# A redrawn order of 3657 operations and fewer early filler matmuls in clustered attention with a softplus feed-forward, on one core

## Chip, core and metric

The kernel runs on one core of one Trainium2 chip. The metric is the device time of one execution in microseconds, as the median of several runs. The core's engines take their instructions each from a queue of its own and wait for each other by semaphores: TensorE (PE, matmuls and transposes), VectorE (DVE), ScalarE (ACT), GpSimd (POOL), and SyncE (SP), which issues the DMAs.

## The reference

Four batches of eight heads, 768 rows of 64, attend within clusters: a row of q and a row of k see each other only if their nearest centroid out of 16 is the same. A feed-forward with softplus follows.

```python
q_assign = np.argmax(np.einsum('bhsd,hcd->bhsc', q_n, c_n), axis=-1)
k_assign = np.argmax(np.einsum('bhsd,hcd->bhsc', k_n, c_n), axis=-1)
mask = q_assign[:, :, :, None] == k_assign[:, :, None, :]
scores = np.where(mask, scale * np.matmul(q, k.transpose(0, 1, 3, 2)), -1000000000.0)
attn = np.exp(scores - np.max(scores, axis=-1, keepdims=True))
attn = attn / (np.sum(attn, axis=-1, keepdims=True) + 1e-09)
x = np.matmul(attn, v)                    # 3072 rows of 512 over all heads
h = x @ w_in                              # 512 -> 2048
g = np.maximum(h, 0.0) + np.log1p(np.exp(-np.abs(h)))
return g @ w_out                          # 2048 -> 512
```

## The kernel before

Numbers are split into a high and a low fp16 part, so that a product in fp32 quality is three fp16 matmuls (high by high, high by low, low by high). A split is two steps that occur all over the program: a cast (`cast`, recorded at L538) makes the high part, and a subtraction (`sub`, L528) makes the low one. `cast` can stand on ACT, DVE or POOL, `sub` on DVE or POOL. The weights arrive as 64-bit floats; `prep_weights` turns them into fp32 by integer steps on DVE and ACT (L662 to L683) and splits them (tiles wi and wo).

The work runs in 8 passes, a half of one batch's rows each (3 tiles of 128 rows for each of 8 heads). For each of 192 score tiles, `scores` does four matmuls (L1020), the negated row maximum on DVE (negm, L1036), the exponential on ACT (p, L1047) and then one of three ways of turning the weights: the first 24 tiles are transposed in fp32 on PE (pT, L1064, then ptf), 10 later ones on PE too (L1087 to L1095), and most of the others are split into phl (`cast`, `sub`) in pairs of tiles, which a transposing DMA on SP brings to pt. `attend` then multiplies with v (tile mbank; L1152 in fp32, L1156 to L1158 in fp16 parts); after the last tile of two heads DVE scales the result by the sums' reciprocals (rs, x, L1182 to L1191), and the result is split (xn) and turned into xT. `ffn1` (L1235 to L1237) makes h, `softplus` makes fg on ACT, DVE and POOL (L1262 to L1284) and splits it into gh, `ffn2` (L1318 to L1320) makes o, and `store` (L1334, L1338, then a DMA) writes it. The keys and queries of the first pass (kn, qn) are transposed on PE (kT, qT, L743) and copied from PSUM by ACT or DVE (`evict`, L519).

What sets the order is written out by hand. Each piece of work is a generator that yields its operations; `Order.run` takes the next code of the table SEQUENCE, its remainder modulo 1000 names the generator whose operation is recorded next, and its thousands name the engine where an operation offers a choice. So the table fixes both each engine's queue and who does each cast, subtraction and copy. The waits between engines follow from the tiles.

`Order` also keeps a clock of planned times. From it `warm` (L484 to L493) puts filler matmuls (128x120, into a bank that nobody reads) on PE where the plan has a gap: 0.9 of the gap in pieces of 52 ns before the plan's time 30000 ns, a share of WARM_SHARE later, where gaps over WARM_FROM alone count.

Of the kernel before, what the change touches and what calls it, by code (L numbers as in the profile page):

```python
# [35 lines left out]
WARM_SHARE = 0.65  # L36
# [368 lines left out]
def tile_cluster_attention__then__softplus_ffn(  # L405
# [80 lines left out]
    def warm(begin, end):  # L486

        ready, spot = min([(od.ev[b], b[1]) for b in od.idle] + [(od.mread, 9)])
        gap = end - max(begin, ready)
        if gap > (150 if begin < 30000 else WARM_FROM):  # L490
            out = idle if spot == 9 else ps_u.tile([P, 512], F32, tag=f"u{spot}", name="fill")[:, :WARM]
            for _ in range(int(gap * (0.9 if begin < 30000 else WARM_SHARE) / 52)):
                nc.tensor.matmul(out, eye, ones[:, :WARM], start=True, stop=True)  # L493
# [858 lines left out]
    first, begin = {}, []  # L1352
# [61 lines left out]
```

## Time and profile before

| what | us |
|---|---|
| median of 3 runs (838.05 to 838.40) | 838.29 |
| the profiled execution | 839.26 |
| its span, first to last instruction of the program | 837.5 |
| PE busy | 819.1 |
| DVE busy | 661.1 |
| ACT busy | 577.7 |
| POOL busy | 410.0 |

A busy time is the union of an engine's instructions; the matmuls' ends are modelled, so PE's is an upper one, and PE's fillers count as busy. The chain of work that ended last runs 74% of the span through PE, 8% through DVE, 7% through ACT and 5% through the transposing DMAs.

### The profile page before, as it was taken

How to read it: one execution, taken by the hardware profiler on the slowest of the kernel's cores; microseconds unless marked ns; L12 is line 12 of the kernel's file. 1: busy time of each engine (PE TensorE's matmuls, PEld its weight loads, DVE VectorE, ACT ScalarE, POOL GpSimd, SP SyncE). 2: the span in 40 equal slices, each digit the busy share in tenths (PEclk: the TensorE clock that was granted, in tenths of full speed). 3: DMA queues.
4: the chain of work that ended last, by engine and by line, in shares of the span. 5: the costliest groups of instructions: out<-in, count | busy, mean ns of one | idle time of the engine just before them, and what ended most of it. 6: DMA issues, size and time to landing. Idle time of an engine off the chain costs nothing.

```text
span 837.5 us, 19752 instructions
## 1 busy us (share of the span) xinstructions
PE 819.1 (98%) x8016; PEld 526.7 (63%) x8016; DVE 661.1 (79%) x1168; ACT 577.7 (69%) x977; POOL 410.0 (49%) x327
## 2 busy tenths in 40 slices
PE   9999989999999999999999999999999999999998
PEld 9788966655666666555565666656666666655553
DVE  7999999999898988889675788888777777534442
ACT  6999989987677758666676656667677587533230
POOL 3334445643554634563565455756566665421220
PEclk9999999999999999999999999999999999999999
DMA  9326887999989999999957999999999985500001
GB/s 328 117 95 141 232 168 190 197 216 191 191 173 181 180 192 190 190 204 174 192 105 108 174 189 201 189 203 207 185 182 181 163 161 113 98 23 13 26 1 38
DMA packets 377003, 131.93 MB, mean 158 GB/s; under 512 B 353360, under 2 KB 369744, under 8 KB 376912
## 3 DMA queue, kind: packets, MB, share of 16 engines
q1 hardware_dynamic: 376912, 130.67, 77.1%
q8 instruction: 62, 1.02, 0.5%
q14 instruction: 29, 0.24, 0.1%
HBM read 35.68 MB, written 6.29 MB: 50 GB/s over the span
## 4 chain that ended last, share of the span: by engine, by line
PE 74%; DVE 8%; ACT 7%; DMA 5%; issue 3%; POOL 2%; POOLq 0%; ACTq 0%; DVEq 0%
PE s L1020 11%; PE o L1318 8%; PE o L1319 8%; PE o L1320 8%; PE h L1235 8%; PE h L1236 8%; PE h L1237 8%; DMA pt<-phl 5%; PE mbank L1156 3%; PE mbank L1158 3%; PE mbank L1157 3%; PE mbank L1152 2%; DVE negm L1036 2%; ACT p L1047 2%; PE pT L1064 1%
## 5 line engine op out<-in xcount | busy, mean ns | idle before, releaser
L1047 ACT ACTIVATE p<-s,negm 128x768 f32<-128x768 f32 x188 | 168.7, 902 | 78.0 <-DVE negm L1036 70.3
L1036 DVE TENSOR_REDUCE negm<-s 128x1 f32<-128x768 f32 x192 | 181.1, 951 | 31.7 <-PE s L1020 28.2
L528 POOL TENSOR_TENSOR phl<-p,phl 128x768 f16<-128x768 f32 x81 | 138.2, 1711 | 79.4 <-ACT phl L538 37.5
L1235 PE MATMUL h<-xT,wi 128*128 128x384 f16 x512 | 166.7, 326 | 1.8 <-DVE fg L1273 1.2
L1237 PE MATMUL h<-xT,wi 128*128 128x384 f16 x512 | 166.8, 326 | 0.0
L1236 PE MATMUL h<-xT,wi 128*128 128x384 f16 x512 | 166.8, 326 | 0.0
L1020 PE MATMUL s<-kt,qt 128*128 128x384 f16 x768 | 156.0, 325 | 2.4 <-ACT p L1047 1.4
L1320 PE MATMUL o<-wo,gh 128*128 128x512 f16 x384 | 145.5, 379 | 0.0
L1319 PE MATMUL o<-wo,gh 128*128 128x512 f16 x384 | 145.5, 379 | 0.0
L1318 PE MATMUL o<-wo,gh 128*128 128x512 f16 x384 | 145.5, 379 | 0.0
L1284 POOL TENSOR_TENSOR fg<-fg,fa 128x384 f32<-128x384 f32 x68 | 74.3, 1094 | 109.8 <-ACT fa L1280 95.3
L1156 PE MATMUL mbank<-vb,pt 128*128 128x65 f16 x1008 | 108.9, 192 | 5.9 <-DMA pt<-phl 4.0
L1157 PE MATMUL mbank<-vb,pt 128*128 128x64 f16 x1008 | 108.9, 192 | 0.0
L1158 PE MATMUL mbank<-vb,pt 128*128 128x65 f16 x1008 | 108.6, 194 | 0.0
L1156 PEld LDWEIGHTS <-pt 128*128 128x128 f16 x1008 | 93.6, 98 | 18.7 <-DMA pt<-phl 7.1
L1157 PEld LDWEIGHTS <-pt 128*128 128x128 f16 x1008 | 93.0, 97 | 13.7 <-issue 2.4
L1020 PEld LDWEIGHTS <-qt 128*128 128x128 f16 x768 | 71.4, 98 | 47.9 <-issue 3.8
L1158 PEld LDWEIGHTS <-pt 128*128 128x128 f16 x1008 | 93.2, 97 | 0.0
L538 ACT CAST phl<-p 128x768 f16<-128x768 f32 x107 | 87.5, 832 | 7.9 <-DMA pt<-phl 6.6
L1266 ACT ACTIVATE fa<-h 128x384 f32<-128x384 f32 x79 | 38.7, 490 | 71.8 <-PE h L1237 65.3
L1279 ACT ACTIVATE fa<-fa 128x384 f32<-128x384 f32 x128 | 66.5, 524 | 27.0 <-DVE fa L1262 26.6
L528 DVE TENSOR_TENSOR phl<-p,phl 128x768 f16<-128x768 f32 x73 | 78.2, 1079 | 6.8 <-ACT phl L538 6.1
(174 smaller groups left out, 1466.2 us busy)
## 6 DMA issues: line engine op xcount, KB each, us to landing
wo<-in_moe_w_in_dram SPq DMA_DIRECT2D x16, 512.0 KB, 7.6
wo<-in_moe_w_out_dram SPq DMA_DIRECT2D x14, 512.0 KB, 4.1
rawk<-in_k_dram SPq DMA_DIRECT2D x16, 384.0 KB, 4.7
rawv<-in_v_dram SPq DMA_DIRECT2D x16, 384.0 KB, 4.2
rawq<-in_q_dram SPq DMA_DIRECT2D x16, 384.0 KB, 4.1
out_dram<-ot SPq DMA_DIRECT2D x24, 256.0 KB, 2.5
pt<-phl SPq DMA_TRANSPOSE x79, 6.0
wraw<-in_moe_w_out_dram SPq DMA_DIRECT2D x2, 512.0 KB, 4.6
```

The costliest lines, as they stand in the source:

```text
L528: [lambda e=e: e.tensor_tensor(dst, a, b, ALU.subtract) for e in (nc.gpsimd, nc.vector)],
L1020: nc.tensor.matmul(st[:, j, :SH], qt[:, s, i], kt[:, s, NT // 2 * j : NT // 2 * (j + 1)], start=(s == 0), stop=(s == 1),)
L1036: yield op("DVE", 950, lambda: nc.vector.tensor_reduce(negm, st[:, :, :SH], AX.XY, ALU.max, negate=True))
L1156: nc.tensor.matmul(av, pt[:, 0, c], vb[:, c, D : 2 * D + 1], start=(c == 0), stop=False)
L1157: nc.tensor.matmul(av[:, :D], pt[:, 0, c], vb[:, c, :D], start=False, stop=False)
L1158: nc.tensor.matmul(av, pt[:, 1, c], vb[:, c, D : 2 * D + 1], start=False, stop=(c == NT - 1))
L1235: nc.tensor.matmul(hp, w[0], x[0], start=(c == 0), stop=False)
L1236: nc.tensor.matmul(hp, w[0], x[1], start=False, stop=False)
L1237: nc.tensor.matmul(hp, w[1], x[0], start=False, stop=(c == NP - 1))
L1318: nc.tensor.matmul(po, g[0], wo[:, f, 0, 0], start=(f == f0), stop=False)
L1319: nc.tensor.matmul(po, g[0], wo[:, f, 0, 1], start=False, stop=False)
L1320: nc.tensor.matmul(po, g[1], wo[:, f, 0, 0], start=False, stop=(f == f0 + NF // 2 - 1))
```

## The change

SEQUENCE is another order of the same operations: 3657 codes in both, 3348 places of which differ. 445 codes choose the second engine of an operation where 459 did, 102 the third where 60 did. In `warm` the first gap (planned to begin before 2500 ns) is filled to 0.95 in pieces of 100 ns, and gaps up to 30000 ns to 0.75 instead of 0.9. The fillers go from 303 to 224, those ahead of PE's first transposes from 89 to 44. Everything else stays.

```diff
@@ -97,170 +97,170 @@
 SEQUENCE = [
-    0, 0, 0, 1, 0, 0, 0, 5, 0, 0, 0, 1, 2, 0, 3, 0, 4, 6, 5, 469, 0, 467, 0, 0, 468, 0, 433, 1001, 471, 8, 1, 0, 9,
+    1, 0, 0, 0, 0, 2001, 0, 0, 0, 5, 0, 0, 0, 0, 0, 2, 0, 3, 1001, 0, 5, 1, 1, 0, 468, 4, 1005, 0, 0, 469, 1, 0, 0,
...
@@ -489,7 +489,7 @@
         gap = end - max(begin, ready)
         if gap > (150 if begin < 30000 else WARM_FROM):
             out = idle if spot == 9 else ps_u.tile([P, 512], F32, tag=f"u{spot}", name="fill")[:, :WARM]
-            for _ in range(int(gap * (0.9 if begin < 30000 else WARM_SHARE) / 52)):
+            for _ in range(int(gap * (0.95 if begin < 2500 else 0.75 if begin < 30000 else WARM_SHARE) / (100 if begin < 2500 else 52))):
                 nc.tensor.matmul(out, eye, ones[:, :WARM], start=True, stop=True)
```

The first place is DVE's queue in the opening, from the last step of the centroids' norms to the first copies of transposed keys (cn and cb are the centroids' parts, kn the first two heads' keys, vb the values, kT the transposed keys in PSUM). Before:

```order
L591 TENSOR_SCALAR cn<-cf,crn 128x64
L594 MEMSET cb 128x192
L528 TENSOR_TENSOR kn_0_138<-rawk_124,kn_0_138 128x12x64
L596 CAST cb<-cn 128x64
L528 TENSOR_TENSOR vb_103<-rawv_128,vb_103 128x12x64
L596 CAST cb<-cn 128x64
L519 COPY kt_139<-kT_0_0_173 128x768
L597 TENSOR_TENSOR cb<-cn,cb 128x64
L921 SCALAR_TENSOR_TENSOR qn_2_0_151<-rawq_0_125,qn_2_0_151 128x6x64
L598 TENSOR_TENSOR cb<-cn,cb 128x64
L921 SCALAR_TENSOR_TENSOR qn_0_0_150<-rawq_0_125,qn_0_0_150 128x6x64
```

Now:

```order
L528 TENSOR_TENSOR kn_0_135<-rawk_124,kn_0_135 128x12x64
L591 TENSOR_SCALAR cn<-cf,crn 128x64
L594 MEMSET cb 128x192
L528 TENSOR_TENSOR vb_103<-rawv_128,vb_103 128x12x64
L596 CAST cb<-cn 128x64 x2
L597 TENSOR_TENSOR cb<-cn,cb 128x64
L598 TENSOR_TENSOR cb<-cn,cb 128x64
L519 COPY kt_136<-kT_0_6_215 128x768
L921 SCALAR_TENSOR_TENSOR qn_0_0_153<-rawq_0_125,qn_0_0_153 128x6x64
L921 SCALAR_TENSOR_TENSOR qn_2_0_154<-rawq_0_125,qn_2_0_154 128x6x64
```

The kn subtraction moves ahead of cn, the two cb subtractions ahead of the first copy out of PSUM, and that copy takes the second half of kT (kT_0_6), the first half being ACT's now.

The second place is DVE's queue at the 33rd to 35th row maximum (wo are weights in preparation, phl_3 a pair of tiles on its way to a transposing DMA). Before:

```order
L1036 TENSOR_REDUCE negm_4_2015<-s_4_2005 128x1
L519 COPY xT_1254<-xT_0_3_2102 128x384
L677 SCALAR_TENSOR_TENSOR wo<-wo 128x512
L683 SCALAR_TENSOR_TENSOR wo<-wo 128x512 x2
L528 TENSOR_TENSOR phl_3_2108<-p_2_3_2097,phl_3_2108 128x768
L528 TENSOR_TENSOR phl_3_2108<-p_2_4_2100,phl_3_2108 128x768
L1273 TENSOR_SCALAR fg_0_2146<-h_0_2110 128x384
L1036 TENSOR_REDUCE negm_5_2134<-s_5_2107 128x1
L1036 TENSOR_REDUCE negm_3_2154<-s_3_2136 128x1
```

Now:

```order
L519 COPY xT_1270<-xT_0_0_1975 128x384
L668 TENSOR_SCALAR wo<-wo 128x512
L519 COPY xT_1270<-xT_0_3_2013 128x384
L1036 TENSOR_REDUCE negm_4_1989<-s_4_1953 128x1
L677 SCALAR_TENSOR_TENSOR wo<-wo 128x512
L528 TENSOR_TENSOR kn_8_1982<-rawk_1897,kn_8_1982 128x12x64
L677 SCALAR_TENSOR_TENSOR wo<-wo 128x512
L1036 TENSOR_REDUCE negm_3_2074<-s_3_2066 128x1
L1036 TENSOR_REDUCE negm_5_2020<-s_5_1988 128x1
```

The two phl_3 subtractions left DVE, for POOL; a kn subtraction and a second copy to xT came to it.

The third place is POOL's queue in the third and fourth pass (phl a pair of tiles, gh and fg the feed-forward, xn attention's result). Before:

```order
L538 CAST gh_4_4488<-fg_4_4291 128x768
L528 TENSOR_TENSOR phl_1_4474<-p_15_1_4410,phl_1_4474 128x768
L528 TENSOR_TENSOR phl_3_4541<-p_8_3_4523,phl_3_4541 128x768
L1284 TENSOR_TENSOR fg_6_4625<-fg_6_4625,fa_12_4624 128x384
L1284 TENSOR_TENSOR fg_6_4625<-fg_6_4625,fa_13_4640 128x384
L528 TENSOR_TENSOR phl_5_4685<-p_9_3_4678,phl_5_4685 128x768
L528 TENSOR_TENSOR gh_6_4754<-fg_6_4625,gh_6_4754 128x768
L1284 TENSOR_TENSOR fg_7_4724<-fg_7_4724,fa_14_4723 128x384
L528 TENSOR_TENSOR phl_4_4793<-p_9_4_4787,phl_4_4793 128x768
```

Now:

```order
L1284 TENSOR_TENSOR fg_5_4413<-fg_5_4413,fa_11_4403 128x384
L538 CAST phl_5_4596<-p_9_3_4599 128x768
L528 TENSOR_TENSOR phl_5_4596<-p_9_3_4599,phl_5_4596 128x768
L538 CAST phl_5_4596<-p_8_5_4545 128x768
L528 TENSOR_TENSOR phl_5_4596<-p_8_5_4545,phl_5_4596 128x768
L528 TENSOR_TENSOR xn_2_4471<-x_13_2_4410,xn_2_4471 128x2x3x64
L1284 TENSOR_TENSOR fg_7_4651<-fg_7_4651,fa_14_4640 128x384
L528 TENSOR_TENSOR phl_4_4692<-p_9_4_4653,phl_4_4692 128x768
L538 CAST phl_4_4692<-p_9_5_4716 128x768
L528 TENSOR_TENSOR phl_4_4692<-p_9_5_4716,phl_4_4692 128x768
```

Where POOL did subtractions alone, it now often does a tile's cast and its subtraction one behind the other.

## Rows read from the trace of the kernel before

**Rows 1.** Busy us, share of the span and instructions of each engine.

```profile
PE 819.1 (98%) x8016; PEld 526.7 (63%) x8016; DVE 661.1 (79%) x1168; ACT 577.7 (69%) x977; POOL 410.0 (49%) x327
```

**Rows 2.** Stretches of the span; columns: us, busy (instructions) by engine, PE clock, DMA.

```profile
0.00:40.00 40.00, 36.50 (x594) 34.04 (x595) 34.20 (x120) 31.41 (x55) 14.35 (x22) 1.00 0.64 231
40.00:95.00 55.00, 54.19 (x502) 48.37 (x501) 54.38 (x102) 54.25 (x116) 22.29 (x22) 1.00 0.52 143
95.00:130.00 35.00, 32.09 (x385) 25.22 (x385) 34.14 (x59) 31.74 (x52) 15.81 (x14) 1.00 0.86 190
130.00:440.00 310.00, 303.70 (x3061) 187.83 (x3059) 275.12 (x458) 232.91 (x379) 164.87 (x125) 1.00 0.94 183
440.00:740.00 300.00, 298.96 (x2999) 184.07 (x2998) 227.16 (x378) 199.31 (x322) 176.18 (x133) 1.00 0.90 165
740.00:837.50 97.50, 93.64 (x485) 47.15 (x483) 36.09 (x54) 28.07 (x57) 16.46 (x14) 1.00 0.06 19
```

**Rows 3.** The same stretches for the fillers of L493 alone (PE, PEld).

```profile
0.00:40.00 40.00, 17.79 (x237) 15.96 (x237) 1.00 0.64 231
...
95.00:130.00 35.00, 4.12 (x66) 3.78 (x66) 1.00 0.86 190
```

**Rows 4.** What PE waited for: us in total, times, longest.

```profile
PE mbank L1156 <- DMA pt<-phl: 4.0, 7, 1.7
PE mbank L1156 <- DVE x L1191: 1.9, 2, 1.1
...
PE h L1235 <- DVE fg L1273: 1.2, 2, 0.9
```

**Rows 5.** Timeline of the opening: start us, length us, engine, line, operation [idle before].

```profile
1.84 7.58 PE L493 MATMUL fill<-ones,eye 128*128 128x120 f16 x89 [1.84 <-DVE ones L465]
...
5.87 0.89 DVE L528 TENSOR_TENSOR kn<-rawk,kn 128x768 f16<-128x768 f32 x1
...
8.12 0.94 ACT L917 ACTIVATE qn<-rawq 128x384 f16<-128x384 f32 x2 [1.58 <-DMA rawq<-in_q_dram]
...
9.26 0.50 PE L743 MATMUL kT<-eye,kn 128*128 128x128 f16 x6
...
9.59 1.79 PE L493 MATMUL mbank<-ones,eye 128*128 128x120 f16 x31
...
9.80 0.56 DVE L519 COPY kt<-kT 128x768 f16<-128x768 f16 x1 [1.97 <-PE kT L743]
```

**Rows 6.** Groups of instructions: count | busy us, mean ns | idle us before them.

```profile
L538 DVE CAST wi<-wo 128x512 f16<-128x512 f32 x7 | 3.6, 508 | 0.0
...
L528 DVE TENSOR_TENSOR phl<-p,phl 128x768 f16<-128x768 f32 x73 | 78.2, 1079 | 6.8 <-ACT phl L538 6.1 <-POOL phl L538 0.2
...
L683 DVE SCALAR_TENSOR_TENSOR wo<-wo 128x512 int32<-128x512 int32 x14 | 9.5, 688 | 0.1
...
L519 DVE COPY qt<-qT 128x384 f16<-128x384 f16 x4 | 1.4, 348 | 0.1
...
L538 DVE CAST phl<-p 128x768 f16<-128x768 f32 x26 | 17.1, 659 | 1.7 <-DMA pt<-phl 0.9 <-issue 0.8
...
L538 POOL CAST phl<-p 128x768 f16<-128x768 f32 x21 | 18.3, 874 | 20.6 <-ACT p L1047 11.0 <-DMA pt<-phl 7.3 <-issue 2.0
...
L1273 DVE TENSOR_SCALAR fg<-h 128x384 f32<-128x384 f32 x65 | 35.8, 550 | 27.9 <-ACT fa L1266 27.9
```

**Rows 7.** Timeline at 356 us on POOL and DVE, then PE's waits there.

```profile
355.95 1.64 POOL L528 TENSOR_TENSOR phl<-p,phl 128x768 f16<-128x768 f32 x1
...
356.02 2.39 DVE L528 TENSOR_TENSOR phl<-p,phl 128x768 f16<-128x768 f32 x1 [0.20 <-POOL phl L538]
...
358.74 0.56 DVE L1191 TENSOR_TENSOR x<-mbank,rs 128x384 f32<-128x384 f32 x1
...
PE mbank L1156 <- DVE x L1191: 1.1, 1, 1.1
```

**Rows 8.** Timeline of DVE's last instruction.

```profile
833.68 0.69 DVE L1338 SCALAR_TENSOR_TENSOR ot<-o,ot 128x512 f32<-128x512 f32 x1 [4.49 <-PE o L1320]
```

326 rows, old and new, of the table SEQUENCE are left out of this document.

## The prediction

> **What bounds the kernel now.** I read the busy times first, then the same busy times cut into stretches, then what TensorE (PE) waited for, then the timeline of the opening, and last single groups of instructions for durations. PE is busy 819.1 of 837.5 us [rows 1], so at most 18.4 us of idle time and whatever PE does that is not the program's own work can be won: 303 filler matmuls (L493), which are busy for 17.79 us in the first 40 us and 4.12 us between 95 and 130 us [rows 3]. The reader is to see in the stretches [rows 2] that the limit changes. In 0 to 40 us PE idles 3.5 us and fills 17.79. From 40 to 95 us PE (54.19 of 55), VectorE (DVE, 54.38) and ScalarE (ACT, 54.25) are all full. From 95 to 130 us DVE is full (34.14 of 35), ACT has 3.3 us free, and PE idles 2.9 and fills 4.12: DVE sets the pace. From 130 to 740 us PE is the limit, with 6.30 and 1.04 us idle; from 740 us on nothing stops it until the last matmul. GpSimd (POOL) is never the limit, 410.0 us busy in all. What PE waits for afterwards is spread over several names, none above 4.0 us in all [rows 4].
>
> The profiled execution took 839.26 us, 1.76 more than its span; the median of the runs is 838.29, 0.97 below it. I make the sum on the span and carry both differences along. A measurement of this kernel can tell about 0.2% from no change, 1.7 us.
>
> **The opening.** Before, PE runs 89 fillers from 1.84 to 9.2 us. The first kn subtraction on DVE starts at 5.87 and takes 0.89, so its transposes could start at about 6.9; they start at 9.26, when the fillers are through, and DVE idles 1.97 us before the copy of their result at 9.80 [rows 5]. The fillers were not covering a gap, they made one. The 89 took 7.58 us, 85 ns each; the next 31 took 1.79 us, 58 ns each: the first ones ran slower than the new count supposes now (100 ns each). The change puts 44 there: 44 x 0.085 to 0.100 = 3.7 to 4.4 us, ending near 6.2, ahead of the subtraction. The cast of kn moves from ACT to POOL (0.874 us for one of its size [rows 6]) with its load no earlier, so the subtraction still ends at about 6.9, and PE is free by then. DVE then has the two cb casts and subtractions done before the first kt copy. By the seventh row maximum (L1036) the order holds 126 DVE instructions in both kernels, worth the same, so nothing else moves here. Gain 9.26 - 6.9 = **2.4 us**. Bounds: 0, if the raw q load that ACT waits for until 8.12 [rows 5] paces everything behind it; 3.5, all of PE's idle time of this stretch.
>
> From 40 to 95 us I take nothing: PE is full there, and what it has lost by 40 us it carries on.
>
> **95 to 130 us.** Counted in the order up to its 34th row maximum, DVE goes from 264 to 257 instructions. Six wi casts leave it (6 x 0.508 = 3.0), two phl subtractions (2 x 1.079 = 2.2) and two weight steps of L683 (2 x 0.688 = 1.4); four copies to qt come (4 x 0.348 = 1.4) [rows 6]. That is 5.2 us off; the other kinds differ by one to three instructions each and I leave them at nothing. ACT does three more wi casts and three fewer wo casts, four fewer qt copies; it has 3.3 us free here. Most of what leaves goes to POOL, which idles more than half of this stretch (15.81 busy of 35) [rows 2]. DVE thus comes earlier by up to 5.2 us to the maxima on which the scores wait, and PE has 2.9 + 4.12 = 7.0 us to win. One of its waits, 1.7 us for a transposing DMA (part of the 4.0 us [rows 4]), starts from DVE's phl subtractions and shrinks only as far as those are earlier than PE. Bounds 0 (ACT takes over as the limit) and 5.2; I take the middle, **2.7 us**, for ACT's row of the stretch lies closest behind DVE's.
>
> **130 to 740 us.** Here 7.3 us of PE idle are left [rows 2]. Over the whole program DVE has 34 instructions fewer: 14 phl casts (14 x 0.659 = 9.2 us), 11 of L1273 (11 x 0.550 = 6.0) and the six wi casts (3.0) make 18.2, and the other kinds nearly cancel. POOL has 39 more, 26 of them phl casts (26 x 0.874 = 22.7 us) [rows 6], the rest at most as long each, so some 31 in all. POOL's idle half covers them. PE's waits that name a DVE instruction of this stretch, x L1191 1.9 and fg L1273 1.2 [rows 4], are 3.1 us; with DVE's load some 3% lower (18.2 of 661.1) I take off somewhat under half, **1.4 us**. Bounds: +5, most of the idle time gone, and -4, new waits of the same size in other places, since every engine's order was drawn anew. The order itself excludes neither.
>
> **The end** is the same on PE instruction for instruction from the last h groups on, and the last store still follows DVE's 0.69 us [rows 8]: nothing.
>
> Sum: 837.5 - 2.4 - 2.7 - 1.4 = 831.0 us of span, + 1.76 = 832.8 for such an execution, and 0.97 less for the median: **831.8 us**. With all bounds at once it would be 824.6 (3.5 + 5.2 + 5 off) to 842.3 (4 on); the forecast's own case, each term between half and one and a half of itself, is 828.5 to 835.
>
> **Rivals.**
> *Lock collisions on POOL's new pairs (slower).* Of 154 phl tiles POOL does cast and subtraction for 31 instead of 10. At 355.95 us POOL starts a 1.64 us subtraction and DVE, 0.07 us later, one that takes 2.39 instead of some 0.95; DVE's x (L1191) comes 1.44 us late and PE waits 1.1 [rows 7]. That is the price of one collision that reaches PE. The Trainium skill, SBUF — State Buffer, section "SBUF: two separate sides", describes the pair of ports that DVE and GpSimd share as an exclusive lock held for a whole instruction, so the loser stops altogether; the trace agrees, 2.39 against 1.64 + 0.95 less the head start of 0.07 = 2.52. By that rule alone, each of POOL's 39 more casts is one more chance to stop DVE. Against it: POOL holds both steps back to back, so fewer hand-offs between the two engines are needed (DVE cast then POOL subtraction falls from 17 tiles to 2), and in the profile most collisions end inside DVE's slack. Six more such waits (6 x 1.1 = 6.6) eat the forecast; ten more give 831.8 + 11 = 842.8, eight 840.6. Chance 0.10, at about 840.5.
> *The loads pace the opening and ACT the rest.* ACT's wait for raw q stays at 8.12 us and its rows of 40 to 95 us are as full as before; then neither term comes: 838. Chance 0.08.
> *The array's clock rises later.* With 45 fillers fewer in front, PE may stand still for half a microsecond before the first transposes; if the slow spacing of 85 to 100 ns lasts on into the transposes and the next 33 fillers, the opening's 2.4 us are given back: 834.2. The granted clock reads 1.00, the 2.4 GHz level, over the whole stretch [rows 2] and does not resolve this. The Trainium skill, TensorE: Matmul & The Clock Gate, section "Part 1: The HAM clock gate", speaks against the change here: activity releases the clock, an idle array gets the slow one. No row of this profile has PE standing idle between 1.84 and 9.26 us. Chance 0.08.
> *More of the waits go.* All of 95 to 130 us (5.2) and most of the later idle time (5) go with the opening's 2.4: 838.3 - 12.6 = 825.7. For it: DVE's load falls throughout. Against it: half of the waits are for DMAs. Chance 0.16.
>
> **How the numbers follow.** The forecast has 0.58. The range should leave out 2 in 10: from 825 to 838 it leaves out the slower rival (0.10), some 0.04 of the low one and the upper half of "nothing" with it, 0.04. Faster by over 0.2% (below 836.6): 0.58 + 0.16 + 0.08 = 0.82. Within 0.2%: the rival of the loads, 0.08. Slower: the collisions, 0.10.
>
> **What would show it.** Right: the first kT transposes at about 7 us instead of 9.26, DVE's 1.97 us wait gone, PE idle plus fillers between 95 and 130 us down from 7.0 to some 4, POOL near 440 us busy and DVE near 643. Wrong: DVE subtractions of 2 us and longer in greater number with PE's waits for DVE above 6 us in 130 to 740 (lock), the first transposes at 9 us (loads), or an even spacing of 100 ns among fillers after 8 us (clock).

## The result and the profile after

The changed kernel took **826.51 us** (median of 4 runs, 824.27 to 829.44) where the kernel before took 838.35 beside it: a ratio of 0.986, 95% interval 0.983 to 0.989. The prediction was 831.8 (825 to 838), faster by over 0.2%. The sign and the range hold, the range by 1.5 us; the gain is 11.8 us where 6.5 were forecast. Measured a second time (c1 below), the same kernel took 824.81 us beside 839.39, just outside the range.

The profiled execution is the fastest of the four, 824.27 us with a span of 822.2, so 15.3 us of span went. The page's busy line, and its chain of work that ended last, by engine:

```profile
PE 811.4 (99%) x7937; PEld 521.8 (63%) x7937; DVE 643.6 (78%) x1134; ACT 563.7 (69%) x972; POOL 445.5 (54%) x366
...
PE 83%; ACT 6%; DVE 4%; DMA 2%; issue 2%; POOL 2%; SPq 1%; ACTq 0%; POOLq 0%
```

DVE and POOL came out as forecast (643 and 440) against [rows 1], and the chain now runs 83% through PE instead of 74%. The stretches of the changed kernel, columns as in [rows 2]:

```profile
0.00:40.00 40.00, 35.96 (x570) 32.71 (x570) 36.94 (x126) 33.74 (x62) 17.68 (x25) 1.00 0.65 232
40.00:95.00 55.00, 54.78 (x506) 49.65 (x505) 52.88 (x97) 54.24 (x112) 26.19 (x27) 1.00 0.59 153
95.00:130.00 35.00, 33.25 (x398) 24.90 (x398) 34.65 (x64) 32.12 (x54) 21.41 (x21) 1.00 0.86 213
130.00:440.00 310.00, 309.29 (x3095) 191.08 (x3093) 262.32 (x436) 229.09 (x380) 193.91 (x152) 1.00 0.97 183
440.00:740.00 300.00, 300.00 (x2975) 184.35 (x2973) 233.63 (x378) 191.59 (x320) 169.37 (x131) 1.00 0.88 162
```

And its fillers (L493) alone in the first three, columns as in [rows 3]:

```profile
0.00:40.00 40.00, 13.26 (x170) 11.45 (x170) 1.00 0.65 232
40.00:95.00 55.00, 0.69 (x10) 0.61 (x10) 1.00 0.59 153
95.00:130.00 35.00, 2.80 (x44) 2.59 (x44) 1.00 0.86 213
```

The yardstick from here on is the time of a stretch that PE gave to none of the program's work: its length less PE's busy time, plus the fillers' busy time. From [rows 2, 3] and the rows above it goes from 21.3 to 17.3 us in the first 40 us, from 0.8 to 0.9 up to 95, from 7.0 to 4.6 between 95 and 130, and from 7.3 (6.30 + 1.04) to 0.7 between 130 and 740 (0.75 in the second profile). That is 13.0 us of the 15.3. After 740 us the idle time is 0.3 longer, and the other 2.6 lie inside what the profile counts as PE's own busy time (819.1 less 21.9 of fillers against 811.4 less 16.75).

What PE waited for between 130 and 740 us in the changed kernel, us in total, times, longest:

```profile
PE s L1020 <- ACT p L1047: 0.3, 1, 0.3
PE sim_k L760 <- ACT fg L1274: 0.3, 1, 0.3
```

The 1.9 us for x and 1.2 us for fg on DVE [rows 4] are gone, and so is every wait there for a transposing DMA, which was 2.3 us of the 4.0 of the whole span. The opening's timeline, as in [rows 5]:

```profile
1.84 4.03 PE L493 MATMUL fill<-ones,eye 128*128 128x120 f16 x44 [1.84 <-DVE ones L465]
5.85 0.96 DVE L528 TENSOR_TENSOR kn<-rawk,kn 128x768 f16<-128x768 f32 x1
6.87 0.51 PE L743 MATMUL kT<-eye,kn 128*128 128x128 f16 x6 [0.99 <-DVE kn L528]
8.11 0.94 ACT L917 ACTIVATE qn<-rawq 128x384 f16<-128x384 f32 x2
8.53 0.56 DVE L519 COPY kt<-kT 128x768 f16<-128x768 f16 x1
```

The first transposes come at 6.87 us instead of 9.26, straight from the kn subtraction, and DVE's 1.97 us wait ahead of its copy is gone. ACT's first work on raw q still starts at 8.11.

### The profile page after: what moved, and what is told of

Same layout as the page of the kernel before. It is cut to its first block, busy times and chain, and to the rows that moved or that the text cites. A ratio compares the mean times of both kernels' runs of the same rounds, so it can differ in the third digit from the quotient of the medians.

```text
span 822.2 us, 19597 instructions
## 1 busy us (share of the span) xinstructions
PE 811.4 (99%) x7937; PEld 521.8 (63%) x7937; DVE 643.6 (78%) x1134; ACT 563.7 (69%) x972; POOL 445.5 (54%) x366
## 4 chain that ended last, share of the span: by engine, by line
PE 83%; ACT 6%; DVE 4%; DMA 2%; issue 2%; POOL 2%; SPq 1%; ACTq 0%; POOLq 0%
PE s L1020 13%; PE o L1318 10%; PE o L1320 10%; PE o L1319 10%; PE h L1235 9%; PE h L1237 9%; PE h L1236 9%; PE mbank L1158 3%; PE mbank L1156 3%; PE mbank L1157 3%; PE mbank L1152 2%; ACT p L1047 2%; DMA rawk<-in_k_dram 1%; DMA pt<-phl 1%; PE pT L1064 1%
## 5 line engine op out<-in xcount | busy, mean ns | idle before, releaser
L1036 DVE TENSOR_REDUCE negm<-s 128x1 f32<-128x768 f32 x192 | 181.0, 948 | 36.0 <-PE s L1020 35.7
L528 POOL TENSOR_TENSOR phl<-p,phl 128x768 f16<-128x768 f32 x81 | 139.9, 1733 | 59.6 <-ACT phl L538 43.4
L1284 POOL TENSOR_TENSOR fg<-fg,fa 128x384 f32<-128x384 f32 x65 | 72.4, 1117 | 70.3 <-ACT fa L1280 70.2
L538 ACT CAST phl<-p 128x768 f16<-128x768 f32 x95 | 78.1, 831 | 14.1 <-DMA pt<-phl 9.7
L528 DVE TENSOR_TENSOR phl<-p,phl 128x768 f16<-128x768 f32 x73 | 79.0, 1091 | 5.1 <-POOL phl L538 3.1
```

The lines of the kernel that those rows point to most:

```text
L528: [lambda e=e: e.tensor_tensor(dst, a, b, ALU.subtract) for e in (nc.gpsimd, nc.vector)],
```

## The experiments

Theory A: the gain is the new order's, and in 130 to 740 us it comes from DVE's lighter load. Theory B: it is the order's, but from where each operation stands and on which engine, not from a load. Theory C: it is the filler rule's. The later theories were made out of what fell.

### The two halves of the change alone

The first kernel has the new order with the old filler line (287 fillers, 81 ahead of the first transposes), the second the old order with the new filler line (233, 48 ahead).

```diff
 a1_seq_only (on the changed kernel)
-... int(gap * (0.95 if begin < 2500 else 0.75 if begin < 30000 else WARM_SHARE) / (100 if begin < 2500 else 52))
+... int(gap * (0.9 if begin < 30000 else WARM_SHARE) / 52)
 a2_fill_only (on the kernel before)
-... int(gap * (0.9 if begin < 30000 else WARM_SHARE) / 52)
+... int(gap * (0.95 if begin < 2500 else 0.75 if begin < 30000 else WARM_SHARE) / (100 if begin < 2500 else 52))
```

> The new order with the old filler rule: 287 fillers, 81 of them ahead of the first kT transposes instead of 44. If fillers that overrun their gap hold back the first transposes (theory of the opening), these start at about 9 us instead of 6.87 and the time is 826.5 + 2.2 = 828.7. If the opening's lead is used up by later waits, 826.5. If the spread of the changed kernel's runs (824.3 to 829.4) comes from the clock falling back where PE idles early, the runs of this kernel lie within 1 us of each other.

> The old order with the new filler rule: 233 fillers, 48 ahead of the first transposes instead of 89. Theory of the opening: first transposes at about 6.9, 838.35 - 2.4 = 835.9. Rival (loads and later waits absorb it): 838.3. Rival (clock): runs up to 5 us apart, the slowest at a lower mean clock.

Measured: the order alone 827.43 us, ratio 0.987 (0.986 to 0.989); the fillers alone 841.43, ratio 1.004 (1.002 to 1.005), so slower by 3 us, where 2.4 us of gain from the opening were expected. Theory C falls as the source of the gain. The stretches of the second, in its profiled execution (838.93 us, below the median), say where an opening's gain is lost again:

```profile
0.00:40.00 40.00, 35.45 (x547) 31.58 (x548) 36.10 (x124) 33.14 (x59) 15.55 (x23) 1.00 0.65 232
...
95.00:130.00 35.00, 33.40 (x406) 25.50 (x406) 34.92 (x62) 32.53 (x53) 17.20 (x15) 1.00 0.84 200
130.00:440.00 310.00, 302.93 (x3055) 187.26 (x3052) 272.74 (x454) 231.88 (x377) 164.13 (x124) 1.00 0.96 182
440.00:740.00 300.00, 298.00 (x2975) 182.96 (x2973) 224.69 (x378) 197.23 (x319) 174.19 (x132) 1.00 0.88 164
```

Its first 40 us lose 18.2 us (40 - 35.45 + 13.65 of fillers) instead of 21.3 and those from 95 to 130 lose 5.7 (35 - 33.40 + 4.12) instead of 7.0, but PE idles 7.07 + 2.00 = 9.1 us between 130 and 740 instead of 7.3, and its own busy time is 2.4 us longer (817.3 less 17.77 of fillers against 797.2). So the span is only 0.4 us shorter (837.1). Why the median lies 2.5 us above this execution, no trace shows. With the new order alone the idle time from 130 to 740 us is 1.70 + 0.39 = 2.1: the order takes 5.2 of the 7.3 us without help of the fillers, and 11.0 us of the time (838.41 less 827.43). Its first transposes start at 8.55 us, where about 9 was expected.

### Other amounts of fillers in the new order

```diff
 a3_more_fill      0.95 if begin < 2500 else 0.75  ->  0.95 if begin < 2500 else 0.95      (260 fillers)
 a4_no_early_fill  if gap > (150 if begin < 30000 else WARM_FROM)  ->  ... and begin >= 30000   (54)
 c2_first_gap_only 0.95 if begin < 2500 else 0.75  ->  0.95 if begin < 2500 else 0.9       (250)
 c1_after_again    the changed kernel, unedited                                           (224)
```

> The changed kernel with 0.95 instead of 0.75 of the gaps filled between the plan's 2500 and 30000 ns (260 fillers instead of 224; the first 44 as they are). If the spread comes from the clock falling back in early idle time: runs within 1 to 2 us, median 824.5 to 825.5. If fillers there only stand in the way: 827 to 828.

> The changed kernel without any filler before the plan's 30000 ns (54 left). If the fillers only stand in the way: 826.5 or 1 us less. If they hold the clock up: the opening's matmuls at twice their spacing, all runs at a mean clock below that of the changed kernel, 830 to 835.

> The changed kernel itself, unedited, once more beside before. Its first runs lay between 824.27 and 829.44 us, a spread of 5.2 us, while the new order with the old filler rule gave 827.43 (826.99 to 828.23). Theory that the order alone brings the gain and the filler rule next to nothing: a median of 826.5 to 828 us here, ratio 0.986 to 0.988, and at least one run above 828.5 if the spread belongs to the kernel. Rival that the filler rule is worth what the first profiled execution shows over the new order with old fillers (822.2 against 826.3 us of span, 4 us): a median near 824, ratio near 0.983.

> The changed kernel with the old share (0.9) in the gaps after the first one; the first gap keeps its new 44 fillers. If fillers are worth nothing either way: 826.5 to 828.3 us, as the new order with all the old fillers (827.43) and with none of the early ones (827.43). If the cut in the first gap is the part of the filler rule that pays, by the some 1.7 us by which the first transposes of keys come earlier than with the old fillers (6.87 against 8.55 us): about 825.7, and the changed kernel beside it the same. If the cut in the later gaps pays: this one about 1 us above the changed kernel.

Measured: 828.10 us, ratio 0.988 (0.987 to 0.989); 827.43, 0.987 (0.986 to 0.988); the changed kernel again 824.81 (823.78 to 827.46), 0.984 (0.982 to 0.986); and 830.09, 0.990 (0.988 to 0.992). In order of their number, 54, 224, 250, 260 and 287 fillers give 827.4, 824.8 to 826.5, 830.1, 828.1 and 827.4 us. That is no slope in either direction. No amount tried beats the changed kernel's, and what an amount does to the time doesn't follow from the time of the fillers themselves. The expectations were missed by c1, for which the theory that the filler rule does next to nothing asked 826.5 to 828 us and a run above 828.5: its 824.81 is nearer to the rival's 824. So in the new order the filler rule may be worth 0.9 to 2.6 us (827.43 less 826.51 and 824.81). The interval of the order alone (0.986 to 0.989) overlaps that of the first measurement and touches that of the second, so this stays open. They were missed too by c2, whose time lies above all that was expected of it, and by a4, for which 830 to 835 was expected if the fillers hold the clock up. Its runs lie within 0.6 us of each other, so early idle time alone doesn't make the changed kernel's spread of 5.2.

c2 shows one way in which a small lag grows. It differs from the changed kernel by 26 fillers in the first 40 us and by nothing behind them; at 161 us it is 0.33 us late (the reduction of sim_q on DVE starts at 161.18 instead of 160.85). Then SP's queue and ACT in the changed kernel, start and length in us, with the wait in brackets:

```profile
158.25 2.88 SPq L562 DMA_TRANSPOSE xT<-xn  x1
162.09 4.59 SPq L562 DMA_TRANSPOSE pt<-phl  x1
...
161.00 0.68 ACT L662 ACTIVATE wo<-wo 128x512 f32<-128x512 f32 x1 [0.42 <-DMA wo<-in_moe_w_out_dram]
168.73 1.56 ACT L538 CAST phl<-p 128x768 f16<-128x768 f32 x2
```

and the same four in c2:

```profile
158.74 3.63 SPq L562 DMA_TRANSPOSE xT<-xn  x1
163.11 6.14 SPq L562 DMA_TRANSPOSE pt<-phl  x1
...
162.22 0.68 ACT L662 ACTIVATE wo<-wo 128x512 f32<-128x512 f32 x1 [1.32 <-DMA wo<-in_moe_w_out_dram]
171.42 1.56 ACT L538 CAST phl<-p 128x768 f16<-128x768 f32 x2 [1.39 <-DMA pt<-phl]
```

The same transposing DMAs hold SP 0.75 and 1.55 us longer in c2, a weight load comes 1.2 us later to ACT (0.9 of it more waiting), and ACT's next phl cast waits 1.39 us for a buffer that a transposing DMA frees. From a lag of 0.33 us has come one of 2.7 (171.42 less 168.73). Some of it reaches PE; its longest wait between 155 and 195 us, where the changed kernel has none:

```profile
PE sim_k L760 <- DVE ot L1334: 1.0, 1, 1.0
```

The second profile of the changed kernel, 0.3 us late at the same place, keeps 0.3 us: its four SP transposes there last within 0.1 us of the first's. That the steps come and go with what meets on the DMA queues fits this, and is not shown. Why c2's 0.33 us tips them and c1's 0.3 doesn't isn't settled.

### VectorE's load

The table's place of each operation stays, and some casts of the second half of the program change engine. In the old order every second of DVE's casts behind place 1100 goes to POOL (24 casts; phl on DVE from 26 to 12, about as the new order has it). In the new order 28 of POOL's go to DVE. In the code `which` is the engine that the table chooses for a cast (0 ACT, 1 DVE, 2 POOL), `n` the place in the table and `ns` the planned times on the three, by which casts of one size are picked out.

```diff
 b1_before_dve_to_pool: in Order.run, on the kernel before
...
+ hit = len(eng) == 3 and which == 1 and ns[1] > 500 and n >= 1100; self.moved += hit
- eng, ns, emit = eng[which], ns[which], emit[which]
+ eng, ns, emit = eng[which], ns[which], emit[2 if hit and self.moved % 2 else which]
 b2_after_pool_to_dve: on the changed kernel, the same with
+ ... which == 2 ...   emit[1 if hit and self.moved % 7 in (0, 2, 5) else which]
```

> The kernel before with 24 of its casts of 768 columns moved from VectorE to POOL after the opening (phl 26 to 12, gh 18 to 10, vb 2 to 0 on VectorE), every place in the order kept. If VectorE's smaller load is what removed PE's idle time between 130 and 740 us (7.3 us to 0.7): idle there falls by 3 to 6 us, 832 to 835. If the place of each operation in the order is what did it: no gain, 838 to 842, since POOL's longer chains were not planned for.

> The changed kernel with 28 such casts moved back from POOL to VectorE (phl 12 to 32, gh 12 to 20 on VectorE), every place kept. If VectorE's load decides: PE's idle time between 130 and 740 us comes back, 5 us or more, 831 to 834. If the places decide: 826.5 to 829, since a cast is shorter on VectorE than on POOL.

Measured: 839.31 us against 838.92, ratio 1.001 (1.000 to 1.002), for b1, and 831.43, ratio 0.992 (0.990 to 0.993), for b2. In b1, between 130 and 740 us:

```profile
130.00:440.00 310.00, 304.01 (x3077) 188.19 (x3075) 270.85 (x446) 233.08 (x380) 177.13 (x135) 1.00 0.95 183
440.00:740.00 300.00, 299.63 (x2985) 184.00 (x2984) 222.93 (x367) 198.93 (x322) 184.80 (x143) 1.00 0.90 165
```

DVE is lighter by 8.5 us than in [rows 2] (493.8 against 502.3), nearly half of the 18.2 that the prediction took off the whole program, and lighter than in the changed kernel (496.0), and PE still idles 6.4 us. (The trace is of an execution of 837.51 us, 1.8 below its median.) Its waits that name DVE there:

```profile
PE mbank L1156 <- DVE x L1191: 1.3, 2, 1.1
PE h L1235 <- DVE fg L1273: 1.3, 2, 0.9
```

The same two places wait as in [rows 4]. And b2:

```profile
130.00:440.00 310.00, 305.22 (x3070) 188.57 (x3068) 268.77 (x444) 226.24 (x375) 179.85 (x137) 1.00 0.94 179
440.00:740.00 300.00, 299.94 (x2974) 184.11 (x2972) 238.84 (x394) 193.24 (x323) 159.28 (x118) 1.00 0.90 165
```

PE's only wait in b2 there that names DVE:

```profile
PE h L1235 <- DVE fg L1273: 0.8, 1, 0.8
```

Here DVE carries 507.6 us, 5.3 more than before, PE idles 4.8 us (in an execution of 828.64 us, 2.8 below the median), and the median is still 7.5 us ahead of the kernel before. b2's time is where the load theory put it (831 to 834) and above the 829 of the place theory, so load put back on DVE in the new order does cost something, or any move does. As the source of the gain theory A falls twice over: a lighter DVE in the old order brings nothing, and the new order with a heavier DVE than before is still far ahead.

### A cast's engine at its place

Two more swaps in the new order: the same 28 casts to ACT, and the six wi casts of the first part back from POOL to DVE.

```diff
 b3_after_pool_to_act: as b2 with ... emit[0 if hit and self.moved % 7 in (0, 2, 5) else which]
 b4_after_wi_to_dve: as b2 with
+ hit = len(eng) == 3 and which == 2 and 400 < ns[1] < 450 and n < 1100
+ ... emit[1 if hit and self.moved <= 6 else which]
```

> The same 28 casts moved from POOL to ScalarE instead. If only VectorE's load decides: 826.5 to 827.5. If any move that the order was not drawn for costs: 829 or more.

> The changed kernel with six wi casts moved from POOL back to VectorE, as the kernel before had them. If VectorE sets the pace before 130 us: 6 x 0.51 = 3.0 us on VectorE, the time 1.5 to 3 us longer, 828 to 829.5. If not: 826.5.

Measured: 836.48 us, ratio 0.997 (0.996 to 0.999), for b3; 828.61, 0.988 (0.987 to 0.990), for b4. ACT has the most room of the three choices after POOL (it is busy 421 of these 610 us), and yet the 28 casts there cost 10 us. What PE waited for most in b3, 130 to 740 us:

```profile
PE h L1235 <- ACT fg L1274: 5.4, 4, 4.3
```

One of these waits for ACT is 4.3 us long. ACT's timeline shows what stands ahead of that fg, one of the casts that were moved:

```profile
327.65 0.83 ACT L538 CAST phl<-p 128x768 f16<-128x768 f32 x1 [3.88 <-DMA pt<-phl]
...
329.92 0.48 ACT L1274 ACTIVATE fg<-h 128x384 f32<-128x384 f32 x1
```

The cast itself takes 0.83 us; it waits 3.88 us for a phl buffer, which a transposing DMA has yet to read, and what stands behind it in ACT's queue waits too. What follows it is in the stretches around 331 us (columns as in [rows 2]; the last three are the granted clock, the DMA share and GB/s):

```profile
320.00:331.00 11.00, 6.68 (x81) 4.32 (x80) 8.20 (x16) 6.88 (x13) 2.94 (x3) 1.00 1.04 198
331.00:334.60 3.60, 3.60 (x12) 1.41 (x11) 0.93 (x1) 1.43 (x3) 3.31 (x4) 0.53 0.89 149
334.60:340.00 5.40, 5.40 (x32) 2.89 (x30) 2.03 (x3) 3.47 (x6) 1.88 (x2) 1.00 0.70 192
```

After 11 us in which PE was busy for 6.68 and stood idle for 4.3 at one stretch, the granted clock reads 0.53, about the 1.2 GHz level, for 3.6 us. At the 6 matmuls a us of the row behind it, the 12 matmuls would have taken some 2.0, so by this estimate the fall cost 1.6 more. The Trainium skill, TensorE: Matmul & The Clock Gate, section "Part 1: The HAM clock gate", says that an idle array is given the slow clock; the trace agrees here, with 0.53 behind that wait.

b4's time is what was expected if DVE sets the pace before 130 us (828 to 829.5). Its 2 us above the first 826.51 lie inside the intervals of the two ratios, but not its 3.8 above the second measurement (0.982 to 0.986); b2's 5 and b3's 10 lie outside both. So theory B stands, and b3 suggests what in a place counts.

### Casts that wait and casts that don't

Theory W: a cast that waits for a phl buffer holds up its engine's queue, which hurts on ACT and not on POOL. Of a pair of tiles the first cast takes the buffer and waits for it, the second finds it taken. So 20 casts go from POOL to ACT at their places, all first ones or all second ones:

```diff
 d1_first_of_pair_to_act (d2_second_of_pair_to_act: the same with == 1)
+ c = cast(phl[:, u, 0], p32, S); c[4]["u"] = u
- yield cast(phl[:, u, 0], p32, S)
+ yield c
...
+ hit = which == 2 and opt.get("u") == 0 and n >= 1100; self.moved += hit
+ ... emit[0 if hit and self.moved <= 20 else which]
```

> The changed kernel with 20 of POOL's phl casts behind place 1100 on ACT, all of them the first of a pair of tiles: these are the ones that wait until a transposing DMA has freed a phl buffer. In the changed kernel POOL waits 24.0 us for that between 130 and 740 us and ACT 9.7; with 28 mixed casts on ACT, ACT waited 21.6 us and the time was 836.5. Theory W (a cast that waits for a buffer holds up everything behind it in its engine's queue; on POOL that hurts nobody, on ACT it holds softplus and the exponentials on which PE waits): ACT's waits for that DMA rise to 18 us or more, POOL's fall below 8, PE idles 5 us or more between 130 and 740 us, time 832 to 837. Rival (the loss is ACT's extra 0.83 us per cast at its place, whichever cast it is): this kernel and the one with the second of each pair lose alike, some 20/28 of 10 us, both near 832 to 834.

> The changed kernel with 20 of POOL's phl casts behind place 1100 on ACT, all of them the second of a pair, which find their buffer taken already and wait for none; as many casts of the same size as in the kernel beside it. Theory W: ACT's waits for the transposing DMA stay near 10 us, PE idles under 3 us between 130 and 740 us, time 825 to 829.5. Rival (load or place on ACT in general): the same loss as with the first of each pair, near 832 to 834.

Measured: 834.83 us, ratio 0.996 (0.995 to 0.997), with the first ones, and 829.78, 0.989 (0.988 to 0.991), with the second ones. What ACT, POOL and then PE waited for between 130 and 740 us, in d1 (its lines behind 1113 are one higher):

```profile
ACT phl L538 <- DMA pt<-phl: 24.1, 19, 3.3
...
POOL phl L538 <- DMA pt<-phl: 7.0, 2, 4.8
...
PE h L1236 <- ACT fg L1275: 4.9, 3, 4.1
```

in d2:

```profile
ACT phl L538 <- DMA pt<-phl: 15.4, 13, 2.9
...
POOL phl L538 <- DMA pt<-phl: 24.6, 9, 6.5
...
PE h L1236 <- ACT fg L1275: 0.8, 3, 0.4
```

and in the changed kernel:

```profile
ACT phl L538 <- DMA pt<-phl: 9.7, 10, 2.7
...
POOL phl L538 <- DMA pt<-phl: 24.0, 10, 7.1
```

The same engine, number and size of casts, and 5 us between them: the rival, that any cast costs ACT alike, falls. The two sets also stand at different places in the order, and part of the 5 us is the clock: behind its wait of 4.1 us d1 has a stretch at a granted clock of 0.69, and d2 has none like it.

```profile
330.00:335.00 5.00, 5.00 (x20) 2.30 (x19) 1.21 (x2) 1.87 (x5) 4.71 (x5) 0.69 0.85 198
```

Theory W's numbers are met by d1, where PE idles 8.8 us. d2 is worse than it allowed: 829.78 us instead of at most 829.5, ACT's waits 15.4 us instead of near 10, PE idle for 4.8 us instead of under 3 (610 less 605.2 of the stretches). So some 3 us over the first 826.51 are left that it doesn't name; c2, which moves no cast at all, is as far off, and ACT waits 16.6 us for these DMAs there.

In the kernel before the same row of POOL reads 7.3 us in 3 waits, and ACT waited 6.9 us for raw q and k, of which the changed kernel has nothing. So the new order lets POOL do much more of the waiting for buffers. That PE's waits of the old order went for this reason is not shown: ACT's own row rises too, from 6.6 to 9.7 us, and in b1 POOL's rises to 13.5 without any gain.

## Why the prediction was right, and where it was short

**The opening** (forecast 2.4, measured 4.0). The mechanism is the one predicted, 6.87 us for "about 7". The term was sized at the first transposes alone; the fillers behind them fell as well, and the rest, 1.6 us, lies there: fillers are 4.5 us less in these 40 us (17.79 to 13.26), idle time 0.5 more. The bound of 3.5, all of PE's idle time, left the fillers out and was passed. Both conditions of the rival of the loads came true, ACT's work on raw q at 8.11 us and ACT's 54.24 of 55 us up to 95; what failed is its step from there to no gain, since the transposes did not wait for that load. But the halves show that this term is no gain by itself: the old order with the opening made shorter by 3.1 us ends 3 us later.

**95 to 130 us** (2.7, measured 2.5: 7.0 to 4.6 us). Right in size. Of the cause, DVE's lighter load, only a part was tested: with the six wi casts back on DVE (b4) this stretch still loses only 4.5 us (35 - 33.27 + 2.80), and 40 to 95 us loses 2.4 instead of 0.9. These casts act earlier than the prediction placed them, where it had taken nothing. And 1.3 of the 2.5 us come in the old order too, with the new filler line alone (7.0 to 5.7). So the size of this term was in part luck.

**130 to 740 us** (1.4, measured 6.6): the step that was mis-sized, with its reason. The prediction took somewhat under half of the waits for DVE, since DVE's load fell by 3%, and left the waits for DMAs, ACT and PE's other releasers as they were. Nearly all went, those that name no DVE instruction too. The step "with DVE's load some 3% lower" is what failed: b1 took nearly half of that load off in the old order, and with it 1.0 us of idle time and nothing of the time. What the runs put in its place is the order itself, 5.2 us of the 7.3 with the old fillers. That it matters in the new order which queue holds the waits for buffers is shown (d1 against d2, 5 us), and a sum of busy times can't show it. What in the order took the old waits away was not tried operation by operation and stays open. The bound of +5, most of the idle time, was passed, and **"More of the waits go"** (825.7, at 0.16) is the case that came nearest; its reason against itself, "half of the waits are for DMAs", was wrong, since those waits went too. The prediction priced POOL's 26 more casts by POOL's idle half, which covered them (363 of 610 us busy), and did not ask what those casts wait for, though [rows 6] show it: POOL's phl casts had 7.3 us of idle time until a transposing DMA.

**The rest.** 2.6 us of PE's own busy time were in no term. The sum on the span: 831.0 - 1.6 (opening) + 0.1 + 0.2 - 5.2 - 2.3 (busy time less end) = 822.2. The median lies 2.2 us above the profiled execution, where 1.0 below was carried along; so it is 5.3 below its forecast, where the profiled execution is 8.5 below its own (832.8).

**The lock.** Collisions did not get rarer or shorter: the phl subtractions on DVE, from the page of the changed kernel,

```profile
L528 DVE TENSOR_TENSOR phl<-p,phl 128x768 f16<-128x768 f32 x73 | 79.0, 1091 | 5.1 <-POOL phl L538 3.1
```

average 1091 ns where they took 1079 [rows 6], and the longest between 130 and 740 us lasts 2.38 us where it lasted 2.39 [rows 7]. Of all DVE's subtractions there, 5 last 2 us or longer where 2 did, so the first half of that rival's sign came. But PE's waits there name no DVE instruction, so the collisions of POOL's new pairs end where DVE has slack; the price of one that does reach PE was not measured apart.

**The clock.** In the profiled execution the first transposes ran at the full rate (6 in 0.51 us, as before). In the second profile of the same kernel (c1) they did not:

```profile
1.83 4.56 PE L493 MATMUL fill<-ones,eye 128*128 128x120 f16 x44 [1.83 <-DVE ones L465]
6.97 0.82 PE L743 MATMUL kT<-eye,kn 128*128 128x128 f16 x6 [0.58 <-DVE kn L528]
8.49 0.50 PE L743 MATMUL kT<-eye,kn 128*128 128x128 f16 x6
9.03 0.56 DVE L519 COPY kt<-kT 128x768 f16<-128x768 f16 x1 [0.44 <-PE kT L743]
```

The 44 fillers took 104 ns each instead of 92, PE stood still for 0.58 us, and six transposes took 0.82 us; the next six ran at the full rate. So this rival came true in part in one of the two traces. Its price was not the 2.4 us that it named: DVE's copy comes 0.5 us later than in the first trace (9.03 against 8.53), 0.1 of it with the kn subtraction, and the execution was 0.5 us longer. What a longer stay at the lower rate costs is in the kernel with no early fillers. The transposes L743 up to 17.6 us, and behind it, in that kernel (ns min/median/max, first and last start):

```profile
L743 PE MATMUL kT<-eye,kn x40: 267/314/314, 6.6 to 17.5; 128*128 128x128 f16 x40
...
L743 PE MATMUL kT<-eye,kn x48: 216/219/314, 17.3 to 40.0; 128*128 128x128 f16 x48
```

They take 314 ns up to 17.5 us and 219 behind, where all of the changed kernel's in its first profile take 216 to 230. The row's granted clock reads 1.00 there all the same (0 to 40 us), so in these traces only the matmuls' own durations tell the rate of the opening. Yet this kernel's time is 827.43, as with 81 fillers in front.

## What to carry to other kernels

Busy times don't say where an operation belongs. Here an operation that waited for a buffer stopped everything behind it in its queue, so give it to the queue with nothing urgent behind it, even where its engine is the slower one, and count the waits of each engine by what ends them before pricing a move. An opening that ends earlier is worth its time only if the stretches behind it keep it, so judge it by the idle time after it, and by more than one amount of fillers.

## What the runs showed of the hardware

- A transposing DMA's hold on SP's queue is no constant: 4.59 and 6.14 us for the same pt, 2.88 and 3.63 for the same xT, in two kernels that differ by 0.33 us of lag there. Two programs alike from 40 us on (c1 and c2, 26 fillers apart) end 5.3 us apart in their medians (824.81 and 830.09, with intervals of the ratio that don't meet), which is over a third of the gain measured beside them (14.6).
- TensorE without early fillers stayed at a lower rate until 17.5 us, by its transposes (314 ns against 219), and the program lost nothing measurable by it against the other amounts of fillers: its first row maximum starts 1.0 us later than the changed kernel's, where with 81 fillers in front it starts 1.8 us later (each from the first L1036 of the trace).
- One stall of 4.3 us in the middle of the program was followed by a fall of the granted clock to 0.53 for 3.6 us, where [rows 2] read 1.00 in every stretch.
